# Attention, a mixture of experts and a last layer in one kernel: narrowing steps placed beside other matmuls, and tiles of the last layer begun in the last half expert

## The chip, the cores and the metric

The kernel runs on one core of a Trainium2 chip. The core's engines run side by side, each with its own queue in order: TensorE (PE: matmuls, and PEld: its weight loads), VectorE (DVE), ScalarE (ACT), GpSimd (POOL) and SyncE (SP), which here issues the DMAs. They meet through semaphores. The metric is the device time of one execution in microseconds, the median of several runs.

## The reference

Three layers follow each other on 1536 tokens of 512 features. All is float32.

```python
a = softmax over kept keys (first n_sink keys, and a window of 128) of q k^T / 8
x = (a @ v), heads side by side                       # 2 x 768 tokens, 8 heads of 64
logits = x @ w_gate                                   # 8 experts
P = np.exp(logits - logits.max())
for _ in range(8):
    P /= P.sum(1, keepdims=True) + 1e-09
    P /= P.sum(0, keepdims=True) + 1e-09
    P *= N / E
for e in range(E):
    h = np.maximum(x @ w1[e], 0.0)                    # 512 -> 1024
    out += P[:, e:e + 1] * (h @ w2[e])                # 1024 -> 512
h = out @ w_in                                        # 512 -> 2048
return (h - np.tanh(h)) @ w_out                       # 2048 -> 512
```

The inputs of the last layer's weights arrive as 64-bit floating point numbers; the kernel narrows them to 32 bits itself.

## The kernel before

Every float32 operand of a matmul is split into two fp32r parts, a high part (ScalarE's copy) and a lower part (the difference, on VectorE or GpSimd). A product of two such operands takes three matmuls: high x high, high x low, low x high.

**Attention** fills the first 130 us. Then come 32 **half experts** (`for u in range(units)`): two batches of 768 tokens, eight experts, two halves of 512 hidden features each. In a half expert the first product x @ w1 is done by a scheme with seven products in place of eight. For two quartets a and b that makes 14 steps named `1a` ... `7b`, six matmuls of 128x384 each; they use the PSUM banks px (2), py (1) and pz (2). ScalarE copies some of these banks to SBUF (`kept`: p1, u2, u3), VectorE adds the copies to other banks (`plus`), and `put` writes h: ScalarE's relu for the high part, VectorE for the lower one. The **second products** h @ w2 stand in the same order as steps: `g0 g1 g2` (first half of the hidden features, tokens 0 to 383), `G0 G1 G2` (the second half into the same banks) and `A3 A4 A5` (both halves, the other tokens). They use three banks pg. After each of G0 to A5 VectorE adds the bank, times the gate's probability, to the output rows (L942); I call this the accumulation. Only then is the bank free.

The string `order` sets the sequence of steps on TensorE, and all other engines get their work in the order in which the loop emits it. At steps 1a and 7a (`places`) the w2 weights are split, ScalarE's cast first and then GpSimd's subtraction of 2.4 us, and GpSimd makes the sums that the seven-product scheme needs (L553). At g2 and the steps behind it the w1 weights of the next half expert are split.

**Narrowing** is a generator of 256 steps on VectorE: 32 pieces of the last layer's weights, eight operations on 128x512 each (L686 to L701). A piece is loaded by a DMA one piece ahead and stored to a scratch tensor by another. `some_narrow(n)` takes up to n steps, at most `budget` in a half expert, from half expert 2 on: one each after 5b, 3a, g0, g1, G0, G1, G2, A3, A4 and A5. It finishes in half expert 28. The **gate** (`gates`) is a generator too; `gate_steps` says at which steps of half experts 0 and 1 it goes on. In half expert 2 VectorE scales the six output rows of batch 0 (L869).

The **last layer** begins after half expert 31. First x2, the six output tiles of a batch, is transposed on TensorE (`x2_tile`) and split. Then 16 steps s run, four parts of the hidden features times two batches times two halves of tokens. A step has four tiles (`g1_unit`: 12 matmuls into one of five banks pa, then five operations each on ScalarE and VectorE for h - tanh(h), and the split of h, whose lower part GpSimd writes, L1023), and three second products (`g2_unit`, 12 matmuls into one of three banks). The second products of step s - 1 stand between the tiles of step s, after f = 1, 2 and 3.

The functions that the change touches, with the line numbers of the profile:

Of the kernel before, what the change touches and what calls it, by code (L numbers as in the profile page):

```python
# [17 lines left out]
P = 128  # L18
# [23 lines left out]
class Kernel:  # L42
# [612 lines left out]
    def narrow_steps(self):  # L655
# [96 lines left out]
    def moe(self, ctx):  # L752
# [15 lines left out]
        with ExitStack() as c:  # L768
            self.mixture(c, gp)
        self.last_layer(ctx, gp)  # L770

    def mixture(self, ctx, gp):
# [7 lines left out]
        tmp = ctx.enter_context(tc.tile_pool(name="tmp", bufs=1))  # L780
        self.nrw = ctx.enter_context(tc.tile_pool(name="narrow", bufs=1))
# [3 lines left out]
        ps_g = ctx.enter_context(tc.tile_pool(name="ps_g", bufs=3, space=PSUM))  # L785
        h, prob = self.h, self.prob
# [70 lines left out]
        gate_steps = {0: "g1 g2 G0 G2 A3 A4 A5", 1: "7a 6b g2 G2"}  # L857
        first_order = "1a L 2a 5a 1b 5b 2b 6a L 7a L 4a 3a 6b L 7b L 4b L 3b g0 g1 g2 G0 G1 G2 A3 A4 A5".split()
        for u in range(units):
# [25 lines left out]
            for step in order if u else first_order:  # L885
# [4 lines left out]
                if kind in "1234567":  # L890
# [3 lines left out]
                    if step in places:  # L894
# [13 lines left out]
                    if step in ("5b", "3a"):  # L908
                        some_narrow(1)
# [35 lines left out]
                if x2s and kind != "g":  # L945
                    self.x2_tile(0, x2s.pop(0), ps_z, "z")
# [3 lines left out]
            assert not fills and not x2s  # L950
# [20 lines left out]
    def last_layer(self, ctx, gp):  # L971

        tc, nc = self.tc, self.nc
        V, G = nc.vector, nc.gpsimd
        self.x2d = gp.tile([P, 4 * TH], F32R, name="x2d")
        tp = ctx.enter_context(tc.tile_pool(name="tanh", bufs=2))
        ps_a = ctx.enter_context(tc.tile_pool(name="ps_a", bufs=5, space=PSUM))
        ps_g = ctx.enter_context(tc.tile_pool(name="ps_g2", bufs=3, space=PSUM))
        kst = gp.tile([P, 3], F32, name="kst")
# [12 lines left out]

        def g1_unit(s, f):

            j, b, c = s // 4, s % 4 // 2, s % 2
            w, x = self.w1_view(64 + 2 * j + f // 2), self.x2(b, c)
            ps = ps_a.tile([P, TH], F32, tag="a", name=self.nm("pa"))
            m = 0
            for kk in range(KD):
                for zw, zx in ((0, 0), (0, 1), (1, 0)):  # L1000
# [94 lines left out]
```

## Time and profile before

| | |
|---|---|
| time, median of 3 runs | 1488.01 us (1487.03 to 1491.36) |
| the profiled execution | 1488.91 us, span 1487.0 us |
| TensorE busy | 1420.0 us, 95% |
| VectorE, ScalarE, GpSimd busy | 1010.4, 704.1, 544.4 us |
| TensorE waiting for ScalarE's copy of a product bank | 42.5 us in 27 times |

The profile shows one execution. A row of the timeline is an instruction, or some like ones in a row, with its start, its duration and, in brackets, how long the engine was idle before it and which instruction ended that; a matmul's duration holds an end that the next one overlaps. A window's row gives its length, then the busy time (and number of instructions) of PE, PEld, DVE, ACT and POOL, then TensorE's granted clock as a share of full speed, the share of the DMA engines that was busy and the rate in GB/s. The windows below begin and end where a half expert's first matmul starts: half expert 1 at 173.47, 2 at 210.01, 3 at 250.42, 8 at 413.85, 9 at 449.66, 16 at 676.61, 29 at 1101.85, 31 at 1163.87. Step 2 of the last layer starts at 1236.00.

### The profile page before, as it was taken

To read this page: it belongs to the slowest core of one execution; us is meant where nothing else is said; L and a number is where in the kernel's file an instruction comes from. 1 tells how busy PE (TensorE), PEld (TensorE's weight loads), DVE (VectorE), ACT (ScalarE), POOL (GpSimd) and SP (SyncE) were. 2 spreads that over 40 slices of the span, in tenths; PEclk is the share of its full clock that TensorE was granted. 3 is DMA by queue.
4 is the path that set the end of the run, shared out by engine and by line. 5 is a ranking of instruction groups with operands and counts; after the bars stand their busy time and mean duration, and the time that the engine had idled before them with its cause. 6 is when DMAs were issued, how large, how long until landed. Compare 5 with 4: busy or idle time off the path is not lost.

```text
span 1487.0 us, 20185 instructions
## 1 busy us (share of the span) xinstructions
PE 1420.0 (95%) x7367; PEld 1241.1 (83%) x7367; DVE 1010.4 (68%) x1939; ACT 704.1 (47%) x1381; POOL 544.4 (37%) x492
## 2 busy tenths in 40 slices
PE   9999998999999999999999999999999989999998
PEld 6667877888888888888888888888889878888887
DVE  6985565777776667767666767766664567777775
ACT  6985433334333343344333334333333367777764
POOL 1111332443363444333344433334443133344422
PEclk9998999999999999999999999999999999999999
DMA  6332113232322232322223232322322211000001
GB/s 139 80 72 73 57 57 106 82 105 84 105 87 86 93 107 83 109 90 81 78 85 120 85 107 80 110 81 86 99 72 71 82 44 31 29 29 15 1 22 64
DMA packets 141865, 114.76 MB, mean 77 GB/s; under 512 B 43840, under 2 KB 113728, under 8 KB 141760
## 3 DMA queue, kind: packets, MB, share of 16 engines
q1 hardware_dynamic: 141472, 113.42, 25.6%
q8 instruction: 59, 0.97, 0.3%
q14 instruction: 46, 0.38, 0.1%
q10 hardware_dynamic: 288, 0.00, 0.0%
HBM read 101.86 MB, written 11.53 MB: 76 GB/s over the span
## 4 chain that ended last, share of the span: by engine, by line
PE 68%; DVE 12%; ACT 8%; issue 6%; POOL 3%; DMA 1%; SPq 0%; POOLq 0%; DVEq 0%; ACTq 0%
PE pg L746 37%; PE px L830 14%; PE pa L1001 6%; PE pz L830 5%; DVE h L805 3%; PE py L830 3%; ACT h L804 2%; ACT u L811 2%; ACT an L297 1%; POOL h L1023 1%; POOL st L553 1%; DVE n L690 1%; DVE n L686 1%; DVE n L699 1%; DVE u L815 1%
## 5 line engine op out<-in xcount | busy, mean ns | idle before, releaser
L746 PE MATMUL pg<-w2b,h 128*128 128x512 f32 x2880 | 693.6, 394 | 8.1 <-POOL w2b L591 3.5
L746 PEld LDWEIGHTS pg<-w2b,h 128*128 128x128 f32 x2880 | 539.9, 189 | 122.8 <-POOL h L1023 8.3
L591 POOL TENSOR_TENSOR w2b<-st,w2b 128x1024 fp32r<-128x1024 f32 x72 | 173.6, 2411 | 618.2 <-ACT w2b L588 618.2
L830 PE MATMUL px<-x7c,w1b 128*128 128x384 f32 x1152 | 235.4, 339 | 42.5 <-ACT u L811 42.5
L830 PEld LDWEIGHTS px<-x7c,w1b 128*128 128x128 f32 x1152 | 202.4, 189 | 57.5 <-ACT u L811 54.3
L553 POOL TENSOR_TENSOR st<-st 128x256 f32<-128x256 f32 x248 | 201.6, 813 | 14.6
L811 ACT COPY p<-px 128x384 f32<-128x384 f32 x64 | 30.7, 479 | 324.9 <-PE px L830 324.9
L942 DVE SCALAR_TENSOR_TENSOR xa<-pg,prob,xa 128x512 f32<-128x512 f32 x174 | 129.8, 747 | 68.4 <-PE pg L746 68.4
L830 PE MATMUL pz<-x7a,w1b 128*128 128x384 f32 x768 | 149.7, 336 | 0.0
L1023 POOL TENSOR_TENSOR h<-y,h 128x384 fp32r<-128x384 f32 x63 | 75.6, 1200 | 192.1 <-ACT h L1022 192.1
L830 PEld LDWEIGHTS pz<-x7a,w1b 128*128 128x128 f32 x768 | 135.3, 189 | 0.0
L588 ACT CAST w1b<-st 128x1024 fp32r<-128x1024 f32 (+1 forms) x132 | 115.9, 947 | 0.0
L591 DVE TENSOR_TENSOR w1b<-st,w1b 128x1024 fp32r<-128x1024 f32 (+1 forms) x95 | 108.2, 1140 | 11.3 <-ACT w1b L588 11.3
L811 ACT COPY u<-px 128x384 f32<-128x384 f32 x128 | 61.2, 478 | 96.1 <-PE px L830 96.1
L815 DVE TENSOR_TENSOR u<-u,pz 128x384 f32<-128x384 f32 x64 | 35.2, 551 | 104.4 <-ACT u L811 104.4
L804 ACT ACTIVATE h<-pz 128x384 fp32r<-128x384 f32 x64 | 31.4, 491 | 135.6 <-DVE pz L815 135.6
L830 PE MATMUL px<-x7a,w1b 128*128 128x384 f32 x384 | 79.5, 342 | 2.7 <-issue 2.7
L1012 DVE TENSOR_TENSOR y<-pa,tq 128x384 f32<-128x384 f32 x64 | 35.7, 557 | 67.7 <-ACT th L1010 67.6
L830 PE MATMUL py<-x7a,w1b 128*128 128x384 f32 x384 | 78.0, 338 | 0.0
L588 ACT CAST w2b<-st 128x1024 fp32r<-128x1024 f32 x72 | 75.2, 1044 | 0.0
L830 PEld LDWEIGHTS px<-x7a,w1b 128*128 128x128 f32 x384 | 69.8, 192 | 5.8 <-issue 3.5
L1001 PE MATMUL pa<-x7a,w1b 128*128 128x384 f32 x384 | 73.2, 343 | 1.4 <-DVE x7a L58 1.4
(156 smaller groups left out, 1918.6 us busy)
## 6 DMA issues: line engine op xcount, KB each, us to landing
st<-in_moe_w_dram SPq DMA_DIRECT2D x128, 256.0 KB, 4.0
st<-in_moe_w_dram SPq DMA_DIRECT2D x64, 512.0 KB, 3.7
n<-in_moe_w_in_dram SPq DMA_DIRECT2D x16, 512.0 KB, 3.7
n<-in_moe_w_out_dram SPq DMA_DIRECT2D x16, 512.0 KB, 3.7
wf_in<-n SPq DMA_DIRECT2D x16, 256.0 KB, 2.1
wf_out<-n SPq DMA_DIRECT2D x16, 256.0 KB, 2.2
st<-wf_in SPq DMA_DIRECT2D x8, 512.0 KB, 3.3
st<-wf_out SPq DMA_DIRECT2D x8, 512.0 KB, 3.6
```

Of the source, the lines that this page charges most:

```text
L553: self.nc.gpsimd.tensor_tensor(out=out, in0=a, in1=b, op=op)
L588: self.nc.scalar.copy(out=hi, in_=src)
L591: (engine or self.nc.vector).tensor_tensor(out=lo, in0=src, in1=hi.bitcast(F32), op=ALU.subtract)
L746: self.nc.tensor.matmul(ps, lhsT=self.h[:, f, zh, n * P : (n + 1) * P], rhs=w2[f // 2][:, zw, f % 2, :], start=start and m == 0, stop=stop ...
L804: nc.scalar.activation(out=h[:, f, 0, tok], in_=src, func=AF.Relu)
L805: V.scalar_tensor_tensor(out=h[:, f, 1, tok], in0=src, scalar=0.0, in1=h[:, f, 0, tok].bitcast(F32), op0=ALU.max, op1=ALU.subtract)
L811: nc.scalar.copy(out=t, in_=ps)
L815: V.tensor_tensor(out=out, in0=t, in1=ps, op=ALU.add)
L830: nc.tensor.matmul(ps, lhsT=q.w[:, sw, zw, kk * P : (kk + 1) * P], rhs=x[:, zx, kk], start=k in (1, 2, 5) and m == 0, stop=m == 5, skip_gr ...
L942: V.scalar_tensor_tensor(out=a, in0=held[n], scalar=prob[:, b * NI + n, e : e + 1], in1=a, op0=ALU.mult, op1=ALU.add)
L1001: nc.tensor.matmul(ps, lhsT=w[:, zw, kk, f % 2 * P : (f % 2 + 1) * P], rhs=x[zx][:, kk], start=m == 0, stop=m == 3 * KD - 1,)
L1023: engine.tensor_tensor(out=ht[:, 1], in0=y, in1=ht[:, 0].bitcast(F32), op=ALU.subtract)
```

## The change

- Narrowing steps stand at 1a and beside second products (`narrow_at`: one at 1a, g2, G0, G1, G2 and A5, two at A3 and A4), none after 5b, 3a, g0 and g1. The budget is 9 in a half expert and 10 in every fourth. The first piece is loaded at the start of half expert 1.
- The gate's last four steps stand at g2, G2 and A4 of half expert 1 and at 1a of half expert 2. The scaling in half expert 2 goes from VectorE to ScalarE, one row each after 2b, 4a, 5b, 3a, 6b and 7b.
- The eight sums for batch 1 (`t_sum`), all in half expert 8 before, stand one each in half experts 5 to 12.
- In half expert 31 the narrowing's SBUF is given to the last layer's tiles. The first four tiles of the last layer stand after G0, G2, A3 and A4, x2 tiles after 3a, 6b, 7b (in the bank py) and A3, A4, A5, the split of the last layer's first w2 parts after 3a and 7b and that of its first w1 part after 6b. Tiles and x2 tiles take the product banks in turn.
- In the last layer the second products of step s stand after tile 2 and 3 of step s + 1 and tile 0 of step s + 2.

```diff
         load(0)
+        yield
         for i in range(32):
...
-        gate_steps = {0: "g1 g2 G0 G2 A3 A4 A5", 1: "7a 6b g2 G2"}
+        gate_steps = {0: "g1 g2 G0 G2 A3 A4 A5", 1: "g2 G2 A4", 2: "1a"}
+        narrow_at = {"1a": 1, "g2": 1, "G0": 1, "G1": 1, "G2": 1, "A3": 2, "A4": 2, "A5": 1}
+        last_at = {"G0": 0, "G2": 1, "A3": 2, "A4": 3}
...
-            if u == 2:
-                for i in range(NI):
-                    V.tensor_scalar(
-                        out=self.acc(0, i), in0=self.acc(0, i), scalar1=prob[:, i, 0:1], scalar2=None, op0=ALU.mult
-                    )
+            scaled = list(range(NI)) if u == 2 else []
+            last = u == units - 1
+            if last:
+                narrow_pool.close()
+                self.tp = ctx.enter_context(tc.tile_pool(name="tanh", bufs=2))
...
-            x2s = list(range(NI)) if u == units - 1 else []
-            budget = 0 if u < 2 or fills else 10
+            x2s = dict(zip("3a 6b 7b A3 A4 A5".split(), range(NI))) if last else {}
+            budget = 0 if u < 2 or fills or last else 9 + (u % 4 == 0)
+            if u == 1:
+                next(narrow)
...
-                        if u == 8:
-                            for i in (0, 1) if step == places[0] else (2, 3):
-                                for k in range(2):
-                                    self.t_sum(1, i, k, G)
+                        if 5 <= u <= 12 and step == places[1]:
+                            self.t_sum(1, (u - 5) // 2, (u - 5) % 2, G)
+                    if last and step in ("3a", "7b"):
+                        for x in self.split2_next():
+                            x()(G)
+                    if last and step == "6b":
+                        self.split1_next()[0]()()
+                    if step in x2s:
+                        self.x2_tile(0, x2s[step], ps_y, "y")
+                    if scaled and step in ("2b", "4a", "5b", "3a", "6b", "7b"):
+                        i = scaled.pop(0)
+                        nc.scalar.activation(
+                            out=self.acc(0, i), in_=self.acc(0, i), func=AF.Copy, scale=prob[:, i, 0:1]
+                        )
...
-                    if step in ("5b", "3a"):
-                        some_narrow(1)
+                    some_narrow(narrow_at.get(step, 0))
                     continue
...
-                if step != "g2":
-                    some_narrow(1)
+                some_narrow(narrow_at.get(step, 0))
...
-                if x2s and kind != "g":
-                    self.x2_tile(0, x2s.pop(0), ps_z, "z")
+                if last and step in last_at:
+                    self.g1_unit(0, last_at[step])
+                if step in x2s:
+                    self.x2_tile(0, x2s[step], *self.next_bank())
...
+    def next_bank(self):
+        self.banks.append(self.banks.pop(0))
+        return self.banks[-1]
...
+        second = {}
+        for s in range(self.steps):
+            for i, (d, f) in enumerate(((1, 2), (1, 3), (2, 0))):
+                second[s + d, f] = s, i
+        for s in range(1, self.steps + 2):
             for f in range(4):
...
+                if (s, f) in second:
+                    self.g2_unit(*second[s, f])
+                if s < 3 and f < 3:
+                    self.x2_tile(1, f + 3 * (s - 1), *self.next_bank())
```

What moves on the engines, at three places. First VectorE among the products of half expert 13, which is like 11. Before, from the put of 4a to the one that ends the products (L686, L699 and L701 are narrowing, L815 the addition, L805 the lower part of h):

```order
L805 SCALAR_TENSOR_TENSOR h<-px_8683,h 128x384
L699 TENSOR_TENSOR n_8611<-n_8611,n_8612 128x512
L815 TENSOR_TENSOR pz_8712<-u_1397_8725,pz_8712 128x384
L805 SCALAR_TENSOR_TENSOR h<-pz_8712,h 128x384
L701 SCALAR_TENSOR_TENSOR n_8613<-n_8381,n_8611 128x512
L686 TENSOR_SCALAR n_8808<-n_8609 128x512
L815 TENSOR_TENSOR u_1409_8818<-u_1409_8818,pz_8772 128x384
L805 SCALAR_TENSOR_TENSOR h<-u_1409_8818,h 128x384
L688 TENSOR_SCALAR n_8808<-n_8808 128x512
L805 SCALAR_TENSOR_TENSOR h<-px_8727,h 128x384
L815 TENSOR_TENSOR pz_8772<-u_1403_8797,pz_8772 128x384
L805 SCALAR_TENSOR_TENSOR h<-pz_8772,h 128x384
```

Now the same stretch, from the put of 4a to the end of the products (in the new numbering L809 is the lower part of h, L819 the addition):

```order
L809 SCALAR_TENSOR_TENSOR h<-px_8674,h 128x384
L819 TENSOR_TENSOR pz_8704<-u_1393_8717,pz_8704 128x384
L809 SCALAR_TENSOR_TENSOR h<-pz_8704,h 128x384
L819 TENSOR_TENSOR u_1401_8801<-u_1401_8801,pz_8764 128x384
L809 SCALAR_TENSOR_TENSOR h<-u_1401_8801,h 128x384
L809 SCALAR_TENSOR_TENSOR h<-px_8719,h 128x384
L819 TENSOR_TENSOR pz_8764<-u_1399_8786,pz_8764 128x384
L809 SCALAR_TENSOR_TENSOR h<-pz_8764,h 128x384
```

The four narrowing operations have left this stretch: the addition for 3a follows directly on the put of 4a. Second, VectorE beside the second products of the same half expert, where they have gone. Before, from g2 to A3 (L591 splits w1, L942 is the accumulation):

```order
L591 TENSOR_TENSOR w1b<-st_0_70,w1b 128x4x256
L690 TENSOR_SCALAR n_8809<-n_8808 128x512
L942 SCALAR_TENSOR_TENSOR xa_65<-pg_8799,prob,xa_65 128x512
L591 TENSOR_TENSOR w1b<-st_0_70,w1b 128x3x256
L692 SCALAR_TENSOR_TENSOR n_8809<-n_8808,n_8809 128x512
L942 SCALAR_TENSOR_TENSOR xa_65<-pg_8823,prob,xa_65 128x512
L591 TENSOR_TENSOR w1b<-st_1_71,w1b 128x4x256
L694 TENSOR_SCALAR n_8810<-n_8809 128x512
L942 SCALAR_TENSOR_TENSOR xa_65<-pg_8848,prob,xa_65 128x512
L697 SCALAR_TENSOR_TENSOR n_8808<-n_8609,n_8810 128x512
L942 SCALAR_TENSOR_TENSOR xa_65<-pg_8888,prob,xa_65 128x512
```

Now the same steps (L687 to L702 are narrowing, L958 the accumulation):

```order
L702 SCALAR_TENSOR_TENSOR n_8624<-n_8385,n_8622 128x512
L591 TENSOR_TENSOR w1b<-st_0_70,w1b 128x4x256
L687 TENSOR_SCALAR n_8850<-n_8620 128x512
L958 SCALAR_TENSOR_TENSOR xa_65<-pg_8788,prob,xa_65 128x512
L591 TENSOR_TENSOR w1b<-st_0_70,w1b 128x3x256
L689 TENSOR_SCALAR n_8850<-n_8850 128x512
L958 SCALAR_TENSOR_TENSOR xa_65<-pg_8806,prob,xa_65 128x512
L591 TENSOR_TENSOR w1b<-st_1_71,w1b 128x4x256
L691 TENSOR_SCALAR n_8851<-n_8850 128x512
L958 SCALAR_TENSOR_TENSOR xa_65<-pg_8830,prob,xa_65 128x512
L693 SCALAR_TENSOR_TENSOR n_8851<-n_8850,n_8851 128x512
L695 TENSOR_SCALAR n_8852<-n_8851 128x512
```

Two narrowing operations stand ahead of the accumulation that frees G0's bank where one stood, and two ahead of A3's. Last, ScalarE in half expert 31, before, from the relu of 3a to the first x2 tile (L804 relu, L811 a bank's copy, L588 a weight cast, L57 the copy of an x2 tile):

```order
L804 ACTIVATE h<-pz_13185 128x384
L811 COPY u_1798_13263<-px_13200 128x384
L811 COPY u_1800_13278<-px_13200 128x384
L804 ACTIVATE h<-u_1800_13278 128x384
L804 ACTIVATE h<-px_13200 128x384
L804 ACTIVATE h<-pz_13241 128x384
L588 CAST w1b<-st_0_70 128x1024
L588 CAST w1b<-st_1_71 128x1024
L57 CAST x7a<-x_1803_13325 128x4x128
```

Now, from the relu of 3a (L808) to the first tile of the last layer (L1029, its first square):

```order
L808 ACTIVATE h<-pz_13194 128x384
L588 CAST w2b_5264<-st_0_5268 128x1024
L57 CAST x7a<-x_1798_13269 128x4x128
L815 COPY u_1799_13282<-px_13209 128x384
L588 CAST w1b<-st_0_70 128x1024
L57 CAST x7a<-x_1800_13287 128x4x128
L815 COPY u_1802_13307<-px_13209 128x384
L808 ACTIVATE h<-u_1802_13307 128x384
L588 CAST w2b_5265<-st_1_5269 128x1024
L57 CAST x7a<-x_1803_13315 128x4x128
L808 ACTIVATE h<-px_13209 128x384
L808 ACTIVATE h<-pz_13250 128x384
```

Between the relu of 3a and the copy of 6b's bank there are now a weight cast and the copy of an x2 tile, and the other casts and copies follow among the products.

## Rows read from the trace of the kernel before

**Rows 1.** Windows at half experts' starts: length, busy us, clock, DMA share, GB/s.
```profile
173.47:210.01 36.54, 33.04 (x168) 28.88 (x166) 25.59 (x63) 12.48 (x21) 12.53 (x11) 1.00 0.18 58
210.01:250.42 40.41, 33.55 (x157) 30.00 (x156) 22.28 (x39) 11.90 (x20) 12.87 (x11) 0.92 0.30 98
250.42:413.85 163.43, 156.39 (x781) 140.15 (x780) 111.79 (x165) 59.51 (x100) 65.30 (x55) 1.00 0.31 94
413.85:449.66 35.81, 33.69 (x161) 29.62 (x159) 25.16 (x34) 11.89 (x20) 23.96 (x19) 0.95 0.27 81
449.66:645.60 195.94, 187.23 (x934) 167.74 (x934) 134.15 (x198) 71.41 (x120) 78.39 (x66) 1.00 0.31 97
676.61:1101.85 425.24, 406.81 (x2030) 364.56 (x2028) 290.38 (x427) 154.71 (x260) 169.81 (x143) 1.00 0.30 92
1101.85:1163.87 62.02, 62.02 (x313) 56.22 (x312) 30.37 (x46) 23.81 (x40) 25.18 (x22) 1.00 0.22 68
1163.87:1236.00 72.13, 65.87 (x337) 58.62 (x336) 43.87 (x74) 43.02 (x80) 23.09 (x16) 0.95 0.19 60
```

**Rows 2.** TensorE's waits: total us, times, longest us.
```profile
PE px L830 <- ACT u L811: 42.5, 27, 6.9
```

**Rows 3.** Timeline of half expert 11: start, us, engine, line, out<-in [idle before].
```profile
524.96 2.40 POOL L591 TENSOR_TENSOR w2b<-st,w2b 128x1024 fp32r<-128x1024 f32 x1
...
525.56 2.09 DVE L690 TENSOR_SCALAR n<-n 128x512 int32<-128x512 int32 x1
...
527.57 0.55 DVE L815 TENSOR_TENSOR pz<-u,pz 128x384 f32<-128x384 f32 x1
```

**Rows 4.** Two narrowing lines: count, ns least/median/most, first and last start.
```profile
L690 DVE TENSOR_SCALAR n<-n x32: 412/421/2086, 230.4 to 1080.1; 128x512 int32<-128x512 int32 x32
...
L692 DVE SCALAR_TENSOR_TENSOR n<-n,n x32: 675/683/1250, 234.4 to 1083.6; 128x512 int32<-128x512 int32 x32
```

**Rows 5.** Timeline of half expert 29 (starts at 1101.85), VectorE and GpSimd.
```profile
1104.22 0.56 DVE L815 TENSOR_TENSOR py<-p,py 128x384 f32<-128x384 f32 x1 [1.42 <-PE py L830]
...
1114.48 3.20 POOL L553 TENSOR_TENSOR st<-st 128x256 f32<-128x256 f32 x4
...
1122.62 0.75 DVE L942 SCALAR_TENSOR_TENSOR xa<-pg,prob,xa 128x512 f32<-128x512 f32 x1
...
1127.62 0.75 DVE L942 SCALAR_TENSOR_TENSOR xa<-pg,prob,xa 128x512 f32<-128x512 f32 x1 [0.94 <-PE pg L746]
...
1130.34 0.75 DVE L942 SCALAR_TENSOR_TENSOR xa<-pg,prob,xa 128x512 f32<-128x512 f32 x1 [1.97 <-PE pg L746]
```

**Rows 6.** Timeline of half expert 31 and of step 3 of the last layer.
```profile
1174.30 1.20 PE L830 MATMUL px<-x7c,w1b 128*128 128x384 f32 x6
...
1194.71 0.59 ACT L57 CAST x7a<-x 128x512 fp32r<-128x512 f32 x1 [2.62 <-PE x L967]
...
1195.33 0.69 DVE L58 TENSOR_TENSOR x7a<-x,x7a 128x512 fp32r<-128x512 f32 x1 [0.30 <-ACT x7a L57]
...
1262.77 0.49 ACT L1008 ACTIVATE tq<-pa 128x384 f32<-128x384 f32 x1 [0.88 <-PE pa L1001]
...
1266.51 0.60 DVE L1017 COPY_PREDICATED y<-mk,pa 128x384 f32<-128x384 int32 x1
```

**Rows 7.** Costliest groups: busy us, mean ns | idle before, releaser and its part.
```profile
L746 PEld LDWEIGHTS pg<-w2b,h 128*128 128x128 f32 x2880 | 539.9, 189 | 122.8 <-POOL h L1023 8.3
...
L588 ACT CAST w2b<-st 128x1024 fp32r<-128x1024 f32 x72 | 75.2, 1044 | 0.0
```

**Rows 8.** Timeline of TensorE in step 4 of the last layer.
```profile
1274.35 3.26 PE L746 MATMUL pg<-w2b,h 128*128 128x512 f32 x12
...
1279.55 2.92 PE L746 MATMUL pg<-w2b,h 128*128 128x512 f32 x12
```

**Rows 9.** Windows around two idle stretches, columns as in rows 1.
```profile
185.00:197.00 12.00, 8.50 (x40) 6.57 (x39) 9.17 (x23) 3.55 (x8) 4.06 (x5) 1.00 0.12 45
439.20:449.70 10.50, 10.47 (x40) 8.57 (x41) 8.23 (x12) 0.00 (x0) 1.85 (x2) 0.84 0.13 38
```

More of the change, by code (lines that the diff above doesn't have):

```diff
@@ L767, in moe @@
             self.stage1_next()
-        with ExitStack() as c:
-            self.mixture(c, gp)
-        self.last_layer(ctx, gp)
+        self.last_constants(gp)
+        self.mixture(ctx, gp)
+        self.last_layer()
     def mixture(self, ctx, gp):
@@ L785, in mixture @@
         ps_g = ctx.enter_context(tc.tile_pool(name="ps_g", bufs=3, space=PSUM))
+        self.banks = [(ps_y, "y"), (ps_x, "x"), (ps_x, "x"), (ps_z, "z"), (ps_z, "z")]
+        self.ps_g = ps_g
         h, prob = self.h, self.prob
@@ L949, in mixture @@
             pending = []
-            assert not fills and not x2s
+            assert not fills
         assert not todo and not deferred and next(narrow, 0) == 0
@@ L969, in x2_tile, with last_constants @@
         self.split(x[0][:, :, tok], x[1][:, :, tok], pt)
-    def last_layer(self, ctx, gp):
-        tc, nc = self.tc, self.nc
-        V, G = nc.vector, nc.gpsimd
+    def last_constants(self, gp):
         self.x2d = gp.tile([P, 4 * TH], F32R, name="x2d")
[L976 to L979, printed above, removed]
+        self.kst = gp.tile([P, 3], F32, name="kst")
@@ L1027, in g2_unit @@
-        def g2_unit(s, i):
-            j, b, c = s // 4, s % 4 // 2, s % 2
-            n = 3 * c + i
-            w2 = [self.w2b[(64 + 2 * j + k) % 4] for k in range(2)]
-            ps = ps_g.tile([P, DM], F32, tag="g", name=self.nm("pg"))
-            self.second(ps, n, range(4), w2, True, True)
-            a = self.acc(b, n)
-            if j == 0:
-                V.tensor_copy(out=a, in_=ps)
-                return
-            cuts = (0, DM // 2, DM) if (s, i) == (steps - 1, 2) else (0, DM)
-            for c0, c1 in zip(cuts, cuts[1:]):
-                V.tensor_tensor(out=a[:, c0:c1], in0=ps[:, c0:c1], in1=a[:, c0:c1], op=ALU.add)
-                if j == 3:
-                    r0 = (b * NI + n) * P
-                    nc.sync.dma_start(out=self.out[r0 : r0 + P, c0:c1], in_=a[:, c0:c1])
@@ new lines, in g2_unit @@
+    def g2_unit(self, s, i):
+        j, b, c = s // 4, s % 4 // 2, s % 2
+        n = 3 * c + i
+        w2 = [self.w2b[(64 + 2 * j + k) % 4] for k in range(2)]
+        nc, V = self.nc, self.nc.vector
+        ps = self.ps_g.tile([P, DM], F32, tag="g", name=self.nm("pg"))
+        self.second(ps, n, range(4), w2, True, True)
+        a = self.acc(b, n)
+        if j == 0:
+            V.tensor_copy(out=a, in_=ps)
+            return
+        cuts = (0, DM // 2, DM) if (s, i) == (self.steps - 1, 2) else (0, DM)
+        for c0, c1 in zip(cuts, cuts[1:]):
+            V.tensor_tensor(out=a[:, c0:c1], in0=ps[:, c0:c1], in1=a[:, c0:c1], op=ALU.add)
+            if j == 3:
+                r0 = (b * NI + n) * P
+                nc.sync.dma_start(out=self.out[r0 : r0 + P, c0:c1], in_=a[:, c0:c1])
@@ L1045, in last_layer @@
+    def last_layer(self):
+        second = {}
[3 more added lines that the diff above has]
+        for s in range(1, self.steps + 2):
             for f in range(4):
-                if s < steps:
-                    g1_unit(s, f)
+                if s < self.steps:
+                    self.g1_unit(s, f)
                     if (s % 4, f) in ((1, 0), (3, 2)):
                         for step in self.split1_next():
-                            step()(G)
-                    if (s % 4, f) in ((1, 2), (2, 2)) or s == 0 and f >= 2:
+                            step()(self.nc.gpsimd)
+                    if (s % 4, f) in ((1, 2), (2, 2)):
@@ L1052, in last_layer @@
                         for step in self.split2_next():
-                            step()(G)
-                elif f == 0:
-                    finish_units()
-                if f >= 1 and s >= 1:
-                    g2_unit(s - 1, f - 1)
-                if s < 2 and f >= 1:
-                    self.x2_tile(1, f - 1 + 3 * s, ps_g)
+                            step()(self.nc.gpsimd)
+                elif (s, f) == (self.steps, 0):
+                    self.finish_units()
+                if (s, f) in second:
+                    self.g2_unit(*second[s, f])
```

93 lines of the change are left out of this document (49 added, 44 removed).

## The prediction

> **What bounds the kernel now.** I read TensorE's waits first, then windows cut at the starts of the half experts, then the timeline of single half experts on all engines. TensorE is the bound and most of its work cannot go: in half experts 29 and 30, which do everything but narrowing, it is busy for the whole of the 62.02 us, 31.01 us each, at granted clock 1.00 [rows 1]. So 31.01 us is what a half expert costs when nothing holds TensorE up, and every window above that is to be explained.
>
> Half experts 3 to 7 take 163.43 us, 9 to 14 195.94, 16 to 28 425.24: some 1.65 us too much in each [rows 1]. The list of waits names one cause, product matmuls waiting for ScalarE's copy of a bank: 42.5 us in 27 times, the longest 6.9 [rows 2]. That is about one for each half expert in which narrowing runs. Half expert 11 shows why [rows 3]. At step 5b VectorE gets the narrowing operation L690, which lasts 2.09 us, while its median is 0.42 [rows 4]. It began 0.60 us after GpSimd's subtraction of 2.40 us and ended 0.3 us after it. Only then (527.57) does VectorE add u into the bank of 3a; ScalarE's relu of that bank follows, and the copy of 6b's bank stands behind the relu in ScalarE's queue. Step 7b cannot write that bank before. What narrowing costs is not its sum: it stands at the one place where GpSimd stretches it and where a copy is queued behind what it delays.
>
> The Trainium skill (SBUF — State Buffer, Who interferes with whom) says that of a VectorE operation in a two-port mode and a GpSimd operation the second to issue is blocked until the first has ended. The trace agrees, 2.09 us against 0.42; were the two to share the bandwidth, the operation would take about 0.84 us and the wait at 7b would hardly exist.
>
> **The change part by part.**
>
> *Narrowing only beside second products.* Nothing is added in number: the same 256 VectorE operations, the same 64 DMAs on SyncE's queue. Nine of them in a half expert (every fourth time ten) go to 1a, g2, G0, G1, G2, A3 and A4 in place of ten. Is there room? In half expert 29 VectorE stands idle 0.94 us before A3's accumulation and 1.97 us before A4's [rows 5], and A5's is like A4's: 4.9 us. The eight operations from g2 to A4 need 4 x 0.42 + 4 x 0.68 = 4.4 us [rows 4], of which six operations' worth stood beside G0 to A5 before without a wait. What stands behind them is the accumulation that frees a second-product bank. With three banks A3 needs the one of G0. That accumulation ends at 1123.37 in half expert 29; A3 begins some 2.9 us before its own accumulation at 1127.62 [rows 5], so at 1124.7. The 1.3 us between are used by two operations of 0.4 to 0.7 us. It fits, narrowly. The one at 1a falls into the 1.42 us that VectorE waits for the first bank to add to [rows 5], ahead of GpSimd's first subtraction, which has to wait for ScalarE's cast. GpSimd ends its row of sums at 1117.68, 15.8 us into the half expert [rows 5]; g2 ends 7 us of second products before A3's accumulation, 18.7 us in. So the new places are free of GpSimd and the operations run at their short time. The DMA that loads a piece is issued eight operations ahead as before, so no operation waits for it; at 1a it stands behind the weight loads on SyncE's queue that wait for GpSimd, some microseconds of the thirty it has. Cost 0. The gain is the excess over 31.01: 163.43 - 155.05 = 8.4, 195.94 - 186.06 = 9.9, 425.24 - 403.13 = 22.1.
>
> *Half expert 8* lasts 35.81 us because eight sums for batch 1 stand on GpSimd at once: 23.96 us busy there against 13 elsewhere, with TensorE idle 2.1 us [rows 1]. Spread over half experts 5 to 12, one sum after 7a lengthens GpSimd's row by 10.9/8 = 1.4 us to 17.2, still ahead of g2. Gain 4.8. Together 45.2 us.
>
> *Half experts 1 and 2.* In 1, two gate steps move from among the products to g2, G2 and A4, and the last to 1a of half expert 2: 36.54 us, of which 3.5 idle [rows 1]. VectorE's chain of a gate step then lies under second products. Bounds of the gain are 3.5 (idle only) and 5.5 (down to 31.01); I take 4.5, since three gate products stay. In 2, 6.9 us go with the wait for the first piece's load, now issued a half expert earlier, and the clock of 0.92 with it [rows 1, 2]. VectorE's six scalings go to ScalarE, 0.59 us each by the nearest row [rows 6], 3.5 us in a queue that holds copies for TensorE. If all of it showed, the gain would be 40.41 - 31.01 - 3.5 = 5.9; if none, 9.4. Only the one after 3a stands just before a copy, so I take 1.0 off: 8.4.
>
> *The opening of the last layer.* Today half expert 31 and the steps up to s = 2 last 72.13 us, of which 6.3 idle and 0.05 x 72 = 3.6 at a lower clock [rows 1]; a group that pauses inside counts as busy, so I take 11 us as lost. The w2 parts are split in step 0, and GpSimd's lower parts of h queue behind them. That goes: they are split at 3a and 7b. New waits come instead. At 3a ScalarE's queue now holds the relu, the w2 cast (1.04 us) and the x2 copy (0.59), then VectorE subtracts (0.69) [rows 6, 7]: with the addition and the relu at half a microsecond each, 3.4 us until the one y bank is free. TensorE has four transposes (0.4) and 6b (1.2 [rows 6]) before the second x2 tile needs that bank: 1.8 us of waiting, with g0 and 7b queued behind. At A5 the sixth x2 tile has to pass the chain of tile (0,3) on VectorE, which ends 4.3 us after ScalarE's first square [rows 6], then A4's x2 subtraction, A5's accumulation and its own, together 6.5 us after that tile's matmuls; TensorE has 0.4 + 2.8 + 0.4 us of work meanwhile, so step 1 starts 2.9 us late. 11 - 4.7 = 6 us gained, between 2 (waits twice as long) and 9.
>
> *Second products a tile later.* The first second product of a step lasts 3.26 us, the next 2.92 [rows 8]: 0.34 us of waiting, for GpSimd's lower part of h by the releaser of the weight loads [rows 7]. With one more tile and one more second product in between this is covered. 14 steps x 0.34 = 4.8. The same order gives the last tile more cover too; I count nothing for it.
>
> *The clock.* The new waits can cost clock. Two idle stretches between 185 and 197, 3.5 us together, left it at 1.00; one of 2.1 us in half expert 8 was followed by 0.84 over 10.5 us, 1.7 us lost [rows 9]. So I count one loss of 1.7 for the two new waits; bounds 0 and 3.4.
>
> [...]
>
> **Sum.** 45.2 + 4.5 + 8.4 + 6 + 4.8 - 1.7 = 67.2 us. From the profiled execution's 1488.91 us (span 1487.0) this leaves 1421.7; that execution stands 0.9 above the median of 1488.01, so the prediction is 1421 us. Its own range by the bounds above is 1411 to 1428.
>
> **Rivals.**
> *The product phase recovers by half.* If what is late at 7b is partly ScalarE's queue and not the narrowing, half of 40 us stays: 1441. Against it: half experts 29 and 30 have the same ScalarE work and no wait. 6%.
>
> *The opening goes wrong.* ScalarE and VectorE carry tiles, x2 parts and accumulations at once in half expert 31; if they fall a tile behind, the 6 us are lost and the clock falls for some microseconds more: 1428 to 1434. For it: the 2.9 us above come out of VectorE's queue alone. 8%.
>
> *The narrowing does not leave the path.* If its data and not its place set its start, only half experts 1, 2 and 8 and the last layer gain: 1461. Against it: L690 began right behind VectorE's work and not behind a DMA. 2%.
>
> *Slower.* Narrowing meets GpSimd beside the second products. It does so if GpSimd's row ends after g2, 2.9 us later than in [rows 5]. Then operations of 0.42 are stretched to as much as 2.09 us [rows 4]; the two before G0's accumulation make A3 late by 3.3 - 1.3 = 2 us, and A5 fares likewise. At 4 us in 25 half experts in place of 1.65 the kernel stands at 1488 + 25 x 2.35 - 24 = 1523. The end of GpSimd's row speaks against it. 3%.
>
> **Chances.** Forecast 81%, rivals 6, 8, 2 and 3. What a measurement of this kernel can tell from no change is 0.3%, 4.5 us; only the slower rival and unknown mishaps get near that bound. Faster 95%, same 2%, slower 3%. The range 1411 to 1436 holds the forecast and the opening's rival.
>
> **What would show it.** Right: half experts 3 to 28 at 31.0 to 31.2 us each; hardly a wait of product matmuls for u; narrowing rows never above 0.7 us; one wait of about 2 us at the x2 tile after 6b and one of about 3 us ahead of step 1; 16.6 us for a step of the last layer where it was 17.0. Wrong: second products waiting for VectorE's accumulation in most half experts, or narrowing rows of 1 us and more beside G0 to G2.

## The result and the profile after

The kernel after takes 1421.64 us (median of 4 runs, 1420.43 to 1423.53), 1489.54 before on the same chip; the ratio is 0.9546 with a 95% interval of 0.9526 to 0.9566. The forecast was 1421. The profiled execution took 1421.67 us, its span is 1419.8.

Windows of the kernel after, cut at the starts of half experts 1, 2, 3, 8, 9, 15, 29 and 31 and of step 2 (columns as in [rows 1]; half experts 15 to 28 are left out):

```profile
173.47:205.30 31.83, 31.83 (x165) 28.88 (x164) 21.23 (x58) 12.51 (x21) 12.58 (x11) 1.00 0.22 66
205.30:237.19 31.89, 31.52 (x160) 28.26 (x158) 20.31 (x38) 15.48 (x26) 12.66 (x11) 1.00 0.30 95
237.19:392.25 155.06, 155.06 (x781) 140.52 (x780) 99.11 (x161) 59.60 (x100) 65.82 (x58) 1.00 0.31 96
392.25:423.27 31.02, 31.02 (x158) 28.10 (x156) 20.55 (x33) 11.92 (x20) 13.55 (x12) 1.00 0.32 103
423.27:609.35 186.08, 186.08 (x938) 168.63 (x936) 119.41 (x193) 71.52 (x120) 79.39 (x70) 1.00 0.32 98
...
1043.53:1105.56 62.03, 62.03 (x313) 56.21 (x312) 37.33 (x61) 23.84 (x40) 25.16 (x22) 1.00 0.27 85
1105.56:1169.44 63.88, 59.84 (x314) 54.49 (x312) 39.05 (x68) 39.28 (x73) 21.36 (x13) 0.97 0.20 66
```

First column against second: from half expert 3 to 30 they are equal, and five half experts take 155.06, six 186.08, 31.01 us each. That is what half experts 29 and 30 took before, which had no narrowing then and have it now. Two rows have a gap between length and TensorE's busy time: half expert 2 with 0.37 us and the last with 4.0, the only one with a granted clock below 1.

The list of TensorE's waits of the kernel after, from half expert 0 on (before: 42.5 us in 27 times, [rows 2]):

```profile
PE px L834 <- issue: 2.8, 1, 2.8
PE x L985 <- DVE x7a L58: 1.8, 1, 1.8
...
PE pa L1019 <- DVE x7a L58: 1.4, 1, 1.4
PE px L834 <- ACT u L815: 1.0, 2, 0.7
...
PE pa L1019 <- ACT x7a L57: 0.7, 1, 0.7
...
PE pa L1019 <- DVE x7c L58: 0.3, 1, 0.3
```

The product matmuls' wait for u is down to 1.0 us in two times. The line with `issue` is the start of half expert 0; the four others are waits for x2, in half expert 31 and behind it.

Two lines of narrowing after, minimum, median and maximum in ns; the first performs the same operation as L690 of before, which reached 2086 [rows 4]:

```profile
L691 DVE TENSOR_SCALAR n<-n x32: 412/418/428, 226.9 to 1075.4; 128x512 int32<-128x512 int32 x32
L693 DVE SCALAR_TENSOR_TENSOR n<-n,n x32: 676/682/692, 228.8 to 1093.7; 128x512 int32<-128x512 int32 x32
```

No narrowing row is stretched any more, anywhere: over all eight lines the longest lasts 0.69 us. TensorE in the opening, where the new waits stand:

```profile
1119.49 0.66 PE L985 MATMUL x<-ident,xa 128*128 128x128 f32 x4 [1.85 <-DVE x7a L58]
...
1150.81 0.44 PE L1019 MATMUL pa<-x7a,w1b 128*128 128x384 f32 x1 [0.74 <-ACT x7a L57]
1152.70 3.44 PE L1019 MATMUL pa<-x7a,w1b 128*128 128x384 f32 x11 [1.45 <-DVE x7a L58]
...
1156.64 2.36 PE L1019 MATMUL pa<-x7a,w1b 128*128 128x384 f32 x12
```

The first wait is the second x2 tile's, behind 6b: 1.85 us, predicted 1.8. The next two stand ahead of step 1, 2.19 us together, predicted 2.9. Behind them eleven matmuls take 3.44 us where later twelve take 2.36: in this execution the clock fell behind the waits ahead of step 1, but not behind the one at 6b. A second profiled execution of the kernel after, taken with g, h and i below, has the same waits to 0.02 us, and there the clock did not fall. From half expert 31 to step 2 it takes 62.40 us in place of 63.88:

```profile
1104.22:1166.62 62.40, 58.38 (x313) 52.79 (x311) 38.84 (x67) 39.08 (x73) 21.19 (x13) 1.00 0.21 68
...
1151.33 2.18 PE L1019 MATMUL pa<-x7a,w1b 128*128 128x384 f32 x11 [1.45 <-DVE x7a L58]
```

A step of the last layer, where [rows 8] had 3.26 us for the first second product:

```profile
1209.51 4.35 PE L1019 MATMUL pa<-x7a,w1b 128*128 128x384 f32 x24
1213.69 2.92 PE L747 MATMUL pg<-w2b,h 128*128 128x512 f32 x12
...
1218.56 2.92 PE L747 MATMUL pg<-w2b,h 128*128 128x512 f32 x12
...
1223.42 2.92 PE L747 MATMUL pg<-w2b,h 128*128 128x512 f32 x12
1226.19 4.35 PE L1019 MATMUL pa<-x7a,w1b 128*128 128x384 f32 x24
```

From tile to tile it is 1226.19 - 1209.51 = 16.68 us, and all three second products last 2.92.

### The profile page after: what moved, and what is told of

Same layout as the page of the kernel before. It is cut to its first block, busy times and chain, and to the rows that moved or that the text cites. A ratio compares the mean times of both kernels' runs of the same rounds, so it can differ in the third digit from the quotient of the medians.

```text
span 1419.8 us, 20214 instructions
## 1 busy us (share of the span) xinstructions
PE 1402.1 (99%) x7367; PEld 1240.7 (87%) x7367; DVE 944.7 (67%) x1933; ACT 707.4 (50%) x1387; POOL 528.6 (37%) x492
## 4 chain that ended last, share of the span: by engine, by line
PE 92%; ACT 3%; DVE 3%; issue 1%; DMA 0%; SPq 0%; DVEq 0%; ACTq 0%
PE pg L747 46%; PE px L834 19%; PE pa L1019 9%; PE pz L834 9%; PE py L834 5%; ACT an L297 1%; PE pt L325 1%; PE sc L267 1%; PE px L356 1%; PE gl L650 1%; PE m L209 0%; DVE an L306 0%; DVE araw L284 0%; ACT at L326 0%; ACT h L808 0%
## 5 line engine op out<-in xcount | busy, mean ns | idle before, releaser
L747 PE MATMUL pg<-w2b,h 128*128 128x512 f32 x2880 | 683.1, 391 | 0.0
L591 POOL TENSOR_TENSOR w2b<-st,w2b 128x1024 fp32r<-128x1024 f32 x72 | 172.8, 2400 | 578.1 <-ACT w2b L588 578.1
L834 PE MATMUL px<-x7c,w1b 128*128 128x384 f32 x1152 | 231.4, 335 | 1.0 <-ACT u L815 1.0
L553 POOL TENSOR_TENSOR st<-st 128x256 f32<-128x256 f32 x248 | 189.4, 764 | 14.6
L815 ACT COPY p<-px 128x384 f32<-128x384 f32 x64 | 30.8, 481 | 324.0 <-PE px L834 324.0
L958 DVE SCALAR_TENSOR_TENSOR xa<-pg,prob,xa 128x512 f32<-128x512 f32 x174 | 129.5, 745 | 37.8 <-PE pg L747 37.8
L819 DVE TENSOR_TENSOR u<-u,pz 128x384 f32<-128x384 f32 x64 | 35.5, 554 | 159.2 <-ACT u L815 159.2
L588 ACT CAST w1b<-st 128x1024 fp32r<-128x1024 f32 (+1 forms) x132 | 116.1, 948 | 0.0
L815 ACT COPY u<-px 128x384 f32<-128x384 f32 x128 | 61.4, 480 | 104.4 <-PE px L834 104.4
L591 DVE TENSOR_TENSOR w1b<-st,w1b 128x1024 fp32r<-128x1024 f32 (+1 forms) x95 | 107.7, 1134 | 2.0 <-ACT w1b L588 1.5
L588 ACT CAST w2b<-st 128x1024 fp32r<-128x1024 f32 x72 | 75.2, 1044 | 0.0
L809 DVE SCALAR_TENSOR_TENSOR h<-u,h 128x384 fp32r<-128x384 f32 x64 | 49.2, 770 | 37.9 <-ACT h L808 37.9
```

The costliest lines, as they stand in the source:

```text
L553: self.nc.gpsimd.tensor_tensor(out=out, in0=a, in1=b, op=op)
L588: self.nc.scalar.copy(out=hi, in_=src)
L591: (engine or self.nc.vector).tensor_tensor(out=lo, in0=src, in1=hi.bitcast(F32), op=ALU.subtract)
L747: self.nc.tensor.matmul(ps, lhsT=self.h[:, f, zh, n * P : (n + 1) * P], rhs=w2[f // 2][:, zw, f % 2, :], start=start and m == 0, stop=stop ...
L809: V.scalar_tensor_tensor(out=h[:, f, 1, tok], in0=src, scalar=0.0, in1=h[:, f, 0, tok].bitcast(F32), op0=ALU.max, op1=ALU.subtract)
L815: nc.scalar.copy(out=t, in_=ps)
```

## The experiments

Each kernel was timed beside the kernel before on the same chip. b, c, d and a ran together, g, h and i too, with the kernel after once more.

**b. Two narrowing steps back among the products.** Does the place cost, or something else that the change did?

```diff
-        narrow_at = {"1a": 1, "g2": 1, "G0": 1, "G1": 1, "G2": 1, "A3": 2, "A4": 2, "A5": 1}
+        narrow_at = {"5b": 1, "3a": 1, "G0": 1, "G1": 1, "G2": 1, "A3": 2, "A4": 2, "A5": 1}
```

> The changed kernel, with one narrowing step put back from 1a to after 5b and one from g2 to after 3a (the number in a half expert stays 9 or 10). Theory A (GpSimd stretches what stands there): the step after 5b lasts about 2 us, product matmuls wait 1.35 to 1.65 us for ScalarE's copy in each of some 27 half experts, those last 32.4 to 32.7 us, and the kernel takes about 1421.6 + 27 x 1.5 = 1462 us. Theory B (only the own time of a VectorE step counts, 0.42 or 0.68 us, against the half microsecond that 7b has to spare): the waits are 0.1 us or less and the kernel takes 1422 to 1425 us.

Measured: 1469.66 us, ratio 0.9881 (0.9865 to 0.9898). Half experts 3 to 30 take 32.6 or 32.9 us, but for half expert 15, which narrows nothing, with 31.01. The wait for u is back. TensorE's waits for it in b, then GpSimd, VectorE, ScalarE and TensorE in half expert 11 of b:

```profile
PE px L834 <- ACT u L815: 42.1, 29, 1.7
...
512.57 2.40 POOL L591 TENSOR_TENSOR w2b<-st,w2b 128x1024 fp32r<-128x1024 f32 x1
513.16 2.35 DVE L693 SCALAR_TENSOR_TENSOR n<-n,n 128x512 int32<-128x512 int32 x1
515.44 0.55 DVE L819 TENSOR_TENSOR pz<-u,pz 128x384 f32<-128x384 f32 x1
516.02 0.49 ACT L808 ACTIVATE h<-pz 128x384 fp32r<-128x384 f32 x1 [3.45 <-DVE pz L819]
516.41 0.47 ACT L815 COPY u<-px 128x384 f32<-128x384 f32 x1
516.94 1.31 PE L834 MATMUL px<-x7c,w1b 128*128 128x384 f32 x6 [1.62 <-ACT u L815]
```

This is the chain of [rows 3] again: the narrowing step begins 0.59 us after GpSimd's subtraction and ends 0.54 us after it, then the addition, the relu, the copy, and TensorE 1.62 us late. Two steps of 0.4 to 0.7 us cost 48 us in the kernel.

**c. The same two steps, with GpSimd's subtraction out of their way.** Is it the meeting, or the step in VectorE's queue? The kernel b, with one more line changed:

```diff
-            places = ("1a", "7a") if u else ("5b", "3a")
+            places = ("1a", "6b") if u else ("5b", "3a")
```

> As the kernel with two steps put back to 5b and 3a, but the second split of w2 and GpSimd's work behind it start at 6b in place of 7a, so that GpSimd's subtraction begins after the two narrowing steps. Theory A: the steps after 5b and 3a last 0.42 or 0.68 us, the wait at 7b is under 0.3 us, half experts take 31.0 to 31.3 us and the kernel 1422 to 1430 us. Theory C (a step among the products is harmful as such, because ScalarE's copy is queued behind what it delays): waits of a microsecond and more stay in each half expert, and the kernel takes 1450 us or more. Not foreseen by either: GpSimd's row ends some 3 us later, near g2, and may stretch the steps beside G0.

Measured: 1428.52 us, ratio 0.9609 (0.9593 to 0.9625). The steps stand where b has them, but the wait for u is nearly gone, and half experts take 31.01 to 31.49 us:

```profile
PE px L834 <- ACT u L815: 1.3, 2, 0.7
```

So the place among the products costs hardly anything by itself; the meeting with the 2.40 us subtraction does. Of b's 48 us all but 7 go when GpSimd is moved and the narrowing stays: 4.0 of the 7 are left in half experts 3 to 30, and in half expert 31 a second x2 tile now waits, 2.2 us.

**d. The eight sums back in half expert 8.** The prediction gave them 4.8 us.

```diff
-                        if 5 <= u <= 12 and step == places[1]:
-                            self.t_sum(1, (u - 5) // 2, (u - 5) % 2, G)
+                        if u == 8:
+                            for i in (0, 1) if step == places[0] else (2, 3):
+                                for k in range(2):
+                                    self.t_sum(1, i, k, G)
```

> The changed kernel with the eight sums for batch 1 all back in half expert 8. This is the slower rival of the prediction in one half expert: GpSimd works on beside the second products while narrowing stands there. Theory A: steps beside g2, G0 and G1 are stretched to 1.2 us and more, second products wait for VectorE's accumulation 2 to 5 us, half expert 8 takes 35 to 39 us and the kernel 1426 to 1430 us. Theory B (narrowing beside second products is covered whatever GpSimd does): half expert 8 stays within 31.0 to 31.5 us and the kernel within 1421 to 1423 us.

Measured: 1421.51 us (2 runs), ratio 0.9559 (0.9540 to 0.9578); half expert 8 takes 31.56 us, 0.55 more. GpSimd and VectorE there, beside G0 and G1:

```profile
412.49 3.16 POOL L644 TENSOR_TENSOR tsum<-xa 128x384 f32<-128x384 f32 x2
413.54 1.25 DVE L689 TENSOR_SCALAR n<-n 128x512 f32<-128x512 f32 x1
414.70 0.74 DVE L960 SCALAR_TENSOR_TENSOR xa<-pg,prob,xa 128x512 f32<-128x512 f32 x1
415.61 2.89 POOL L644 TENSOR_TENSOR tsum<-xa,tsum 128x384 f32<-128x384 f32 x2
416.39 1.23 DVE L691 TENSOR_SCALAR n<-n 128x512 int32<-128x512 int32 x1
```

Narrowing meets the sums, and its rows grow from 0.42 to 1.25 us. Without narrowing among the products the sums are worth 0.55 us and not 4.8: the rows are theory A's, the time is nearly theory B's.

**a. The narrowing table alone, in the kernel before.**

```diff
+        narrow_at = {"1a": 1, "g2": 1, "G0": 1, "G1": 1, "G2": 1, "A3": 2, "A4": 2, "A5": 1}
...
-            budget = 0 if u < 2 or fills else 10
+            budget = 0 if u < 2 or fills or u == units - 1 else 9 + (u % 4 == 0)
...
-                    if step in ("5b", "3a"):
-                        some_narrow(1)
+                    some_narrow(narrow_at.get(step, 0))
...
-                if step != "g2":
-                    some_narrow(1)
+                some_narrow(narrow_at.get(step, 0))
```

> The kernel before with only the narrowing steps moved (1a, g2, G0, G1, G2, A3 twice, A4 twice, A5; budget 9 or 10); the first load, the gate, the sums in half expert 8, the opening and the order of the last layer stay. Theory A: half experts 3 to 7, 9 to 14 and 16 to 28 at 31.0 us, 40 us gained there; half expert 8 not better than before (36 to 39 us), since four steps meet GpSimd beside the second products; half expert 2 near 40 us, since the first step still waits for its load. Together 1489.5 - 40 + 0 to 3 = 1449 to 1453 us. Theory B (place does not matter, the number of steps does): 1480 us or more.

Measured: 1443.81 us, ratio 0.9719 (0.9699 to 0.9739), better than expected, since half expert 8 came down with it, to 31.57 us, its sums untouched. Half experts 3 to 28 take 31.01 else, 1 takes 36.56 as before. 2 takes 42.57, 2.2 more than before: its first narrowing step now stands at 1a, ahead of all of VectorE's work for the products, and its wait for the load, which only the full change issues earlier, holds TensorE for 9.9 us in place of 6.9.

**g. Second products a tile earlier again.**

```diff
-            for i, (d, f) in enumerate(((1, 2), (1, 3), (2, 0))):
+            for i, (d, f) in enumerate(((1, 1), (1, 2), (1, 3))):
```

> The kernel after, with the second products of a step after tiles 1, 2 and 3 of the next step, as before. Theory A (the first second product of a step waits 0.34 us for GpSimd's lower part of h, and the extra tile covers that): 14 x 0.34 = 4.8 us are lost again, and some 0.7 at the end, 1427 us; the first second product of a step lasts 3.26 us again. Theory B (the 4.8 us came from elsewhere, such as the w2 casts that no longer stand in ScalarE's queue in step 0 or tiles moved into half expert 31): the last layer's steps stay at 16.7 us and the time at 1421 to 1423 us.

Measured: 1425.28 us (1421.64 to 1425.88), ratio 0.9571 (0.9550 to 0.9591), 4.3 above the kernel after on that chip (1420.95, 1419.09 to 1421.66). The intervals of the ratios overlap, so the trace has to decide. A step of g on TensorE:

```profile
1207.03 4.35 PE L1019 MATMUL pa<-x7a,w1b 128*128 128x384 f32 x24
1211.21 3.25 PE L747 MATMUL pg<-w2b,h 128*128 128x512 f32 x12
...
1224.01 4.35 PE L1019 MATMUL pa<-x7a,w1b 128*128 128x384 f32 x24
```

16.98 us, and the first second product at 3.25 again: theory A, by the rows. From half expert 31 to the end g takes 318.6 us, the kernel after 314.2 and, in its second execution, 313.0; g and the first of these both lose clock in the opening, so 4.3 us is the fair difference.

**i. The splits of w2 late again, after A3 and A4 of half expert 31.**

```diff
-                    if last and step in ("3a", "7b"):
-                        for x in self.split2_next():
-                            x()(G)
...
+                if last and step in ("A3", "A4"):
+                    for x in self.split2_next():
+                        x()(G)
```

> The kernel after, with the splits of the two w2 parts after A3 and A4 of half expert 31 (after: after 3a and 7b). Theory A (before's opening lost its time to GpSimd's lower parts of h queuing behind the w2 parts, so the early split is what gained): the second products of step 0 or the tiles of step 1 wait 2 us and more again, 1424 to 1428 us. Theory B (the tiles moved into half expert 31 gained it, and the early w2 cast only lengthens ScalarE's queue at 3a): the wait at the x2 tile after 6b falls from 1.85 to about 0.8 us and nothing comes in its place, 1420 us.

Measured: 1419.18 us, ratio 0.9536 (0.9519 to 0.9554), not to be told from the kernel after. From half expert 31 to step 2 it takes 63.46 us where the kernel after takes 63.88; the wait behind 6b falls from 1.85 to 0.90, but 0.5 comes back ahead of step 1 (1.67 and 1.05 in place of 0.74 and 1.45). No wait for GpSimd's w2 part returns. So the early split gained nothing, against the prediction's reason for the opening ("That goes: they are split at 3a and 7b"). What did must be in the rest of the change, above all in the tiles moved into half expert 31 or the later second products; no run takes either back together with the early split, so which of them is not shown.

**h. x2 tiles earlier, w2 splits where ScalarE is free.**

```diff
-            x2s = dict(zip("3a 6b 7b A3 A4 A5".split(), range(NI))) if last else {}
+            x2s = dict(zip("3a 7b 3b G1 G2 A3".split(), range(NI))) if last else {}
...
-                    if last and step in ("3a", "7b"):
-                        for x in self.split2_next():
-                            x()(G)
...
+                if last and step in ("G1", "A5"):
+                    for x in self.split2_next():
+                        x()(G)
```

> The kernel after, with the x2 tiles of half expert 31 after 3a, 7b, 3b, G1, G2 and A3 (after: 3a, 6b, 7b, A3, A4, A5) and the splits of the two w2 parts after G1 and A5 (after: 3a and 7b). Theory A: the three waits of the opening (1.85 us at the x2 tile after 6b, 0.74 and 1.45 us in step 1) come from where the x2 tiles and w2 casts stand, the last x2 subtraction behind the chain of tile (0,3) on VectorE. Moved earlier, all three go, and the half clock that follows them (about 1.5 us) with them: 1421.6 - 4.1 - 1.5 = 1416 us, step 2 of the last layer starts at about 1164 where it was 1169.4. Theory B: the y bank and VectorE's queue are the limit wherever the tiles stand, and the waits only move (at 7b, G1 or at step 1's second products, where GpSimd's part of w2 is then late): 1420 to 1423 us.

Measured: 1415.19 us (1414.57 to 1415.52), ratio 0.9511 (0.9496 to 0.9526); every run of it is under every run of the kernel after on that chip. Its window from half expert 31 to step 2:

```profile
1104.35:1161.94 57.59, 57.59 (x313) 52.90 (x311) 38.42 (x67) 39.15 (x73) 21.21 (x13) 1.00 0.22 74
```

63.88 has become 57.59, all of it busy, at clock 1.00: the three waits (4.0 us) and the slow matmuls behind them are gone. Some 1.5 of the 6.3 us is clock that the kernel after keeps as well in its second execution (62.40 us). h beats both kernels.

**j. GpSimd's second subtraction just ahead of g2.** This and the next were to measure the slower rival.

```diff
-            places = ("1a", "7a") if u else ("5b", "3a")
+            places = ("1a", "3b") if u else ("5b", "3a")
```

> The kernel after, with the second w2 split and GpSimd's work behind it after 3b, just ahead of g2, where they stood after 7a: GpSimd's 2.40 us subtraction and its sums now run beside the narrowing steps of g2, G0 and G1. Theory A (the slower rival as the prediction priced it): narrowing rows of 2 us and more there, the accumulations of G0 and G1 late by more than the 1.3 us that are spare, second products of A3 and A5 waiting, half experts of 33 to 35 us and 1480 to 1523 us. Theory B (from the kernel with the sums back in half expert 8, where the rows grew to 1.25 us only and 0.55 us was lost): single rows up to 2 us, but beside second products VectorE's slack takes most of it, half experts of 31.0 to 31.7 us and 1421 to 1443 us.

Measured: 1551.27 us, ratio 1.0420 (1.0396 to 1.0443), outside of both theories. TensorE's first waits in j:

```profile
PE pg L747 <- POOL w2b L591: 58.7, 30, 2.0
PE pg L747 <- ACT w2b L588: 21.5, 30, 0.7
```

The w2 part that is split here is read by G0 of the same half expert. The experiment moved a due time, not only a meeting, and says nothing of the rival.

**k. The same after 7b**, early enough for G0.

```diff
-            places = ("1a", "7a") if u else ("5b", "3a")
+            places = ("1a", "7b") if u else ("5b", "3a")
```

> The kernel after, with the second w2 split and GpSimd's sums behind it after 7b, where they stood after 7a, so that the w2 part is ready before G0 and only GpSimd's sums run beside g2, G0 and G1 and their narrowing steps. Theory A (the slower rival as the prediction priced it): the rows grow to 1.2 to 2.1 us, the accumulations of G0 and G1 are late by more than the 1.3 us that are spare, second products of A3 and A5 wait for VectorE, half experts of 32 to 33 us and 1450 to 1480 us. Theory B (VectorE's slack beside second products takes rows of up to 1.25 us): half experts of 31.0 to 31.5 us, no wait for an accumulation, 1421 to 1436 us. Either way a wait of second products for GpSimd's w2 part at G0 would be the place's own fault and is counted apart.

Measured: 1452.50 us, ratio 0.9762 (0.9738 to 0.9785): 31 us slower than the kernel after, 31.8 to 32.6 us for half experts 3 to 30, but for half expert 15. GpSimd, VectorE and TensorE in half expert 6 of k:

```profile
353.58 4.70 POOL L553 TENSOR_TENSOR st<-st 128x256 f32<-128x256 f32 x4
353.61 1.26 DVE L700 TENSOR_TENSOR n<-n,n 128x512 f32<-128x512 f32 x1
354.79 1.76 DVE L591 TENSOR_TENSOR w1b<-st,w1b 128x1024 fp32r<-128x1024 f32 x1
356.47 1.22 DVE L702 SCALAR_TENSOR_TENSOR n<-n,n 128x512 int32<-128x512 int32 x1
357.62 0.74 DVE L958 SCALAR_TENSOR_TENSOR xa<-pg,prob,xa 128x512 f32<-128x512 f32 x1
358.41 1.89 PE L747 MATMUL pg<-w2b,h 128*128 128x512 f32 x7 [0.54 <-DVE xa L958]
```

Two narrowing steps of 1.2 us in place of 0.68, and VectorE's split of w1 between them (1.76 us, 1.23 in the kernel after), make the accumulation of G0 late, and A3 waits 0.54 us for its bank: the slower rival's mechanism, at its place. The group of the weight loads of second products over all of k, then the window of half expert 15, which narrows nothing:

```profile
L747 PEld LDWEIGHTS pg<-w2b,h 128*128 128x128 f32 x2880 | 532.6, 188 | 142.3 <-DVE xa L958 21.6 <-POOL w2b L591 16.3 <-DVE xa L951 0.9
...
623.65:655.35 31.70, 31.59 (x158) 27.94 (x157) 20.46 (x29) 17.05 (x27) 14.80 (x11) 1.00 0.24 73
```

21.6 us of the waits stand behind accumulations, 16.3 behind the w2 part, which is still late for G0's later matmuls. By this share, an estimate, 4/7 of the 31 us are late accumulations, some 0.6 us in a half expert. Not all of that is narrowing's: half expert 15 takes 31.7 us too, 0.7 more than in the kernel after, with other steps of VectorE beside GpSimd's sums; the others lose 1.1 us on the mean. So 0.6 us is the most that this share leaves for narrowing's meeting with the sums.

## Why the prediction was right

By the two profiled executions, 1488.91 - 1421.67 = 67.2 us, which is the predicted sum. That it agrees to a tenth is luck: the medians differ by 67.9 us on this chip and by 66.6 on the one of g, h and i, and errors in single terms cancel.

| term | predicted | measured |
|---|---|---|
| half experts 3 to 30 | 45.2 | 913.45 - 868.37 = 45.1 |
| half expert 1 | 4.5 | 36.54 - 31.83 = 4.7 |
| half expert 2 | 8.4 | 40.41 - 31.89 = 8.5 |
| half expert 31 to the end | 6 - 1.7 + 4.8 = 9.1 | 323.1 - 314.2 = 8.9 |

*Half experts 3 to 28.* The mechanism was that of the trace: GpSimd's subtraction stretches a narrowing step, and a copy stands behind it. b and c show it, one by bringing it back, the other by taking away the meeting alone. The Trainium skill (SBUF — State Buffer, Who interferes with whom) says that the two engines share one pair of ports, which an operation that uses it holds like an exclusive lock; the 2.35 us in b agree, and the 1.25 us in d and k agree too, where what runs on GpSimd are sums of 1.2 to 1.6 us each on the mean. In these rows the price of a meeting is thus about what is left of the GpSimd operation that it meets.

*Half expert 8* was put down to one cause, the sums, where it takes two: a removed its loss by moving the narrowing alone, with the sums in place, but for 0.55 us. The wait differs from that of its neighbours; in the kernel before it is for an accumulation, and the clock behind it is 0.84 [rows 9]:

```profile
439.23 10.06 PE L746 MATMUL pg<-w2b,h 128*128 128x512 f32 x36 [2.12 <-DVE xa L942]
449.13 1.23 PE L830 MATMUL px<-x7a,w1b 128*128 128x384 f32 x6
```

The second row is the first matmul of half expert 9, which thus starts at 449.13 and not at 449.66: half expert 8 took 35.28 us and lost 4.3, not 4.8, and 9 to 14 lost 10.4, not 9.9. The sum of both is the same. Its neighbours took 32.7 us on the mean, so the sums cost some 2.6 us where narrowing steps stand among the products, and 0.55 where they don't.

*Half experts 1 and 2* came within 0.2 us. That of ScalarE's six scalings only one would show fits the single wait left there, 0.37 us, where 1.0 was taken off. What the early load and the move of the scalings gave in half expert 2 each, no run separates.

*The opening.* The x2 wait behind 6b was 1.85 us (1.8 predicted), the one ahead of step 1 2.19 (2.9). That one of the two cost clock, as counted, is luck: the second execution of the kernel after has the same waits and no such loss. What gained was misread: not the early split of w2, which i takes back at no loss.

*Second products.* 17.00 - 16.68 = 0.32 us a step, 14 times is 4.5 of the 4.8. The end, counted at nothing, gave some 0.7: the last 48 matmuls of the kernel before take 11.76 us, the last 60 of the kernel after 13.80, 0.23 each. But g, which takes the order back, loses 4.3 in all, so part of this is lost again, 0.3 of it at an x2 wait in step 2. The opening therefore gave 8.9 - 4.3 = 4.6 net, where 6 - 1.7 = 4.3 was predicted, and 1.3 more in the execution that kept its clock.

*The slower rival* was priced too high. It took the 2.09 us of the 2.40 us subtraction for steps that could only have met sums; the subtraction cannot stand beside second products, because its result is due at G0 (j). With 1.25 us in place of 2.09, and at most 0.6 us lost in a half expert (k) rather than 4, the rival would have given at most 1421 + 28 x 0.6 = 1438 and not 1523, an estimate. That it did not come was right for the reason given: in half expert 11 of the kernel after GpSimd's row ends at 502.09, and g2 begins at 502.67.

## What to carry to other kernels

Look for an operation whose maximum is several times its median and read what the other engine on the same memory does at that moment; what it costs is the rest of that operation, and only where a queue behind it feeds the bound. Either partner can be moved, but the due time of what it makes comes first. When work is moved into a stage that was full, place each tile by the engine that has to empty its bank: three waits that were foreseen to within a microsecond could be placed away for 5.8 us (h).

## What was not expected of the hardware

The clock after a short wait is not settled by its length. In the opening of the last layer two executions with the same waits differed in clock. Half expert 0 shows it too. It has nearly the same waits in every execution, 2.4 to 2.8 us at its start and 0.66 us that ends at 149 or 150; it took 42.1 us in h and 45.4 in i, at a mean clock of 0.92 and 0.85. Five microseconds each from 145 on, of the kernel after and then of i:

```profile
145.00:150.00 5.00, 4.54 (x31) 4.45 (x30) 3.16 (x7) 2.93 (x6) 1.79 (x4) 1.00 0.29 103
150.00:155.00 5.00, 4.79 (x33) 4.79 (x34) 2.02 (x5) 1.65 (x4) 4.76 (x5) 1.00 0.27 77
```

```profile
145.00:150.00 5.00, 4.34 (x29) 4.25 (x28) 2.60 (x6) 2.58 (x5) 1.95 (x2) 1.00 0.13 52
150.00:155.00 5.00, 5.00 (x26) 5.00 (x25) 2.16 (x5) 1.49 (x3) 4.16 (x5) 0.60 0.40 105
```

After the same wait the clock stays at 1.00 in one and falls to 0.60 in the other. The 3.3 us between 42.1 and 45.4 are about as much as the runs of the kernel after differ by (1420.43 to 1423.53), and no edit of h or i is in half expert 0. The Trainium skill (TensorE: Matmul & The Clock Gate, Loop structure matters more than you think) has a long wait of TensorE for a DMA drop the clock to half; here a wait of 0.66 us, not a long one, was followed by a drop in i and not in the kernel after.
